# An FFT mixing layer fused with a squared-ReLU feed-forward: FFT units in half-slots of their own, and the read of a z quarter moved ahead of the read of u

## The chip, the cores and the metric

The kernel runs on one core of one Trainium2 chip. The metric is device microseconds of an execution; the time of a version is the median of its runs. A profile records one execution, with the span from its first to its last instruction.

## The reference

The input is `x` of 8 batches, 3008 positions and 256 channels. Per batch the layer computes

```
X = rfft(x, axis=1); y = irfft(X * (filt_r + 1j*filt_i), n=3008, axis=1)
h = relu(y @ w_in)            # 256 -> 2048
out = (h * h) @ w_out         # 2048 -> 256, over all 24064 tokens
```

All inputs and the output are float32; the kernel works in float16 with float32 accumulation.

## The kernel before

The transform of length 3008 is split as 64 x 47. For each batch it has four kinds of unit, each of which fills one PSUM bank on TensorE (PE) and is emptied by another engine:

- `unit_a` (16 per batch, L345): one 512-column matmul of `x` into `psA`, cast to `u` by ScalarE (ACT) or, for odd units of batches 1 and 2, VectorE (DVE). Four units fill a chunk of `u`, which `write_u` sends to DRAM (`dU`).
- `unit_b` (12, L436): two 256-column matmuls of `ut` into `psB`; DVE multiplies by the filter into `prod` (L450), and GpSimd (POOL) issues two DMAs that add one half of `prod` onto the other (L457).
- `unit_p` (12, L480): two 256-column matmuls of `prod` into `psP`, cast to `ze` by ACT (L489). Every third one sends a quarter of `ze` to DRAM (`dZ`, L492).
- `unit_y` (16, L509): four 94-column matmuls of `zt` into `psY`, cast to `yt` by ACT for even units and by DVE for odd ones (L530, L532).

`read_u` (L429) reads the whole of a batch's `dU` back as `ut`, transposed, in a DMA of 512 KB and one of 1024 KB. `read_z` (L501) reads one quarter of a batch's `dZ` in two DMAs of 192 KB, into one of two buffers. The quarters 0 and 1 of `dZ` are written early, so only the second DMA of a read needs the last write of `dZ`. The reads, the writes of `dU` and `dZ` and all stores of the output are issued on one queue, that of SyncE (SP), in program order; an issue that has to wait holds up what is behind it. The loads of `x` (L195) and the additions onto `prod` stand on POOL's queue.

The feed-forward works on groups of 512 tokens, eight slots to a group. In each slot `ffn_g1` makes two of the 16 tiles of `h` (four matmuls of 512 columns into `psH`, L553; ACT applies the ReLU, L557), and DVE squares them two slots' worth at a time (L564, in every odd slot). The second product of the previous group is done in the same slot: for most groups by `products` (L666), a Strassen form of 16 matmuls of 128 columns per slot into `psX` and `psY`, for which DVE makes four sums (L639 to L648, in slots 0, 1, 2 and 4 of a group) and three additions; for the first groups and the last by `ffn_g2` (L573).

The order of all this is written out by hand. The main loop goes over slots and emits, in each: `ffn_g1`, the units of the slot's first half (place 0), `products` or `ffn_g2`, the units of the second half (place 1), then the sums and the square. Which unit stands in which half is decided by `fft_plan(b)`: it gives each unit a position in slots, counted from a first slot of its batch, and rounds it down to a half-slot. Several units may fall into one half-slot. A batch takes 47 to 48 slots, and the batches overlap: while the last units of batch b run, those of b+1 and b+2 have begun.

All four kinds of unit share two PSUM banks, the tag `psF` with two buffers: a unit can start only when the unit two before it has been emptied.

Of the kernel before, what the change touches and what calls it, by code (L numbers as in the profile page):

```python
# [19 lines left out]
TG = 512  # L20
SLOTS = 8
# [89 lines left out]
def kernel(  # L111
# [9 lines left out]
    nc = tc.nc  # L121
    B, S, D = x.shape
# [564 lines left out]
                nc.vector.tensor_add(out=v, in0=o, in1=v)  # L687
                store(g, 0, 2, f["top"])

    def fft_plan(b):  # L690

        plan = {}

        def put(r, f, *a):
            r = int(2 * r)
            plan.setdefault(divmod(r, 2), []).append((f, a))

        d = 0
        if b == 1:
            for n in range(4, 16):  # L700
                put((n if n < 8 else n + 2 if n < 12 else 2 * n - 7) + n % 2 / 2, unit_y, 0, n)
            put(7.5, read_z, 0, 3)
            for k in range(4):
                put((4.5, 5.5, 7.5, 7.5)[k], cast_wout, k, nc.vector)
            for a in range(12, 16):
                put(2 + a / 2, unit_a, b, a)
            put(10.5, read_u, b)
            d = 7
        else:
            for a in range(16):  # L710
                if a % 2 == 0 and b > 2:
                    put((-57 + 2.3 * a) if b == 3 else (-66 + 2.75 * a), load_x, b, a // 2)
                put((-16 + a, -46 + 2.2 * a, -56 + 2.75 * a)[min(b, 4) - 2], unit_a, b, a)
            put(2 if b == 2 else -9, read_u, b)
        for p in range(12):
            r = 14 + 15 * p / 11 if b == 1 else 6 + 28 * p / 11 if b == 2 else -5 + 39 * p / 11
            put(r, unit_b, b, p)
            if b == 1 and 2 <= p < 10:
                put(r, load_x, 2, p - 2)
            put(r + 4.5, unit_p, b, p)  # L720
        for c in range(4):
            put((41, 41.5, 48, 54)[c] - d, read_z, b, c)
        for n in range(16):
            put(YN[n] - d, unit_y, b, n)
        return plan

    YN = (45, 45.5, 46, 46.5, 47.5, 49, 50.5, 52, 54, 56, 58, 60, 63, 66, 69, 72)

    def run(plan, r, place):
        for f, a in plan.get((r, place), ()):  # L730
            f(*a)


# [8 lines left out]
    for k in range(2):  # L742
        c = slice(12 * k, 12 * k + 12)
# [26 lines left out]
    for k in range(6):  # L770
        if k % 3 == 0:
            sSPx.append(p_u.tile([128, 12, 128], F16, tag="u", name=f"sSPx_{k}"))
        c, o = slice(4 * k, 4 * k + 4), slice(4 * k % 12, 4 * k % 12 + 4)
# [27 lines left out]
    read_z(0, 2)  # L801

    SEVEN = range(6, NG - 1)
    work = {}
    for b in range(1, B):
        first = (b * S // TG) * SLOTS - (48 if b > 1 else 40)
        for (r, place), w in fft_plan(b).items():
            work.setdefault((first + r, place), []).extend(w)

    for s in range((NG + 1) * SLOTS):  # L810
        g, k = divmod(s, SLOTS)
        if g < NG:
            ffn_g1(g, k)
        run(work, s, 0)
        if SEVEN[0] * SLOTS <= s < SEVEN[0] * SLOTS + 4:
            make_t(s % SLOTS)
        if (s - 1) // SLOTS - 1 in SEVEN:
            products((s - 1) // SLOTS - 1, (s - 1) % SLOTS)
        if g > 0 and g - 1 not in SEVEN:
            ffn_g2(g - 1, k)  # L820
        run(work, s, 1)
        if g > 0 and g - 1 not in SEVEN:
            ffn_out(g - 1, k)
        if g - 1 in SEVEN:
            sums(g - 1, k)
        if g < NG:
            ffn_sq(g, k)
# [30 lines left out]
```

## Time and profile before

| | |
|---|---|
| median of 6 runs | 786.99 us (785.86 to 788.06) |
| the profiled execution's own time | 787.4 us |
| its span | 785.4 us |
| PE busy | 755.9 us (96%) |
| DVE, ACT, POOL busy | 618.9 (79%), 583.3 (74%), 193.0 us (25%) |
| DMA | 109.21 MB, mean 139 GB/s |
| granted TensorE clock | 1.000 |

In a timeline each line has a start, a duration, the engine, the source line and what is written from what; in brackets stand the idle time before it and what ended that. A table of windows gives the busy time of each engine in each stretch of the span. A wait has the engine and line that waited, what it waited for, and then the total in us, the number of times and the longest. SPq and POOLq are issues of DMAs, not their transfers.

### The profile page before, as it was taken

How to read it: one execution, taken by the hardware profiler on the slowest of the kernel's cores; microseconds unless marked ns; L12 is line 12 of the kernel's file. 1: busy time of each engine (PE TensorE's matmuls, PEld its weight loads, DVE VectorE, ACT ScalarE, POOL GpSimd, SP SyncE). 2: the span in 40 equal slices, each digit the busy share in tenths (PEclk: the TensorE clock that was granted, in tenths of full speed). 3: DMA queues.
4: the chain of work that ended last, by engine and by line, in shares of the span. 5: the costliest groups of instructions: out<-in, count | busy, mean ns of one | idle time of the engine just before them, and what ended most of it. 6: DMA issues, size and time to landing. Idle time of an engine off the chain costs nothing.

```text
span 785.4 us, 19161 instructions
## 1 busy us (share of the span) xinstructions
PE 755.9 (96%) x8022; PEld 553.6 (70%) x8022; DVE 618.9 (79%) x679; ACT 583.3 (74%) x831; POOL 193.0 (25%) x260
## 2 busy tenths in 40 slices
PE   8989999999989999899999999999998999999998
PEld 5846666667767777777768777687776877777776
DVE  5866655579778888888887899779977999878874
ACT  3976767778867887778877887778786777777774
POOL 3801640133213321222221323233311222000000
PEclk9999999999999999999999999999999999999999
DMA  9995896656775547665486554855537533421011
GB/s 364 372 254 161 149 174 182 171 103 117 153 187 128 107 97 185 163 129 100 105 215 133 112 125 98 206 131 115 105 83 189 125 68 77 116 69 55 28 49 61
DMA packets 104942, 109.21 MB, mean 139 GB/s; under 512 B 9640, under 2 KB 93096, under 8 KB 102936
## 3 DMA queue, kind: packets, MB, share of 16 engines
q1 hardware_dynamic: 85704, 87.38, 36.6%
q0 software_dynamic: 19008, 20.43, 19.4%
q8 instruction: 63, 1.03, 0.5%
q10 hardware_dynamic: 144, 0.18, 0.1%
q14 instruction: 23, 0.19, 0.1%
HBM read 58.12 MB, written 48.23 MB: 135 GB/s over the span
## 4 chain that ended last, share of the span: by engine, by line
PE 82%; DMA 6%; DVE 6%; ACT 2%; SPq 2%; issue 1%; ACTq 0%; DVEq 0%
PE psH L553 35%; PE psX L666 16%; PE psY L666 12%; PE psO L573 6%; DMA zt<-dZ 4%; DVE prod L450 3%; PE psA L358 3%; PE psP L487 2%; PE psY L523 2%; PE psB L442 2%; DVE h L564 1%; PE warm L272 1%; ACT h L557 1%; DMA ut<-dU 1%; PE psf L291 1%
## 5 line engine op out<-in xcount | busy, mean ns | idle before, releaser
L557 ACT ACTIVATE h<-psH 128x1024 f16<-128x1024 f32 x376 | 385.0, 1025 | 156.5 <-PE psH L553 152.4
L553 PE MATMUL psH<-yt,sWin 128*128 128x512 f16 (+7 forms) x1728 | 386.7, 351 | 1.5 <-DVE yt L532 0.6
L564 DVE TENSOR_TENSOR h<-h 128x2048 f16<-128x2048 f16 (+1 forms) x192 | 229.7, 1197 | 68.9 <-ACT h L557 68.6
L457 POOL DMA_DIRECT2D prod<-prod x168 | 138.9, 972 | 463.5 <-DVE prod L450 457.5
L553 PEld LDWEIGHTS <-sWin 128*128 128x128 f16 x1728 | 152.8, 98 | 97.0 <-issue 3.8
L666 PEld LDWEIGHTS <-sum 128*128 128x128 f16 x2560 | 158.0, 98 | 25.2 <-issue 1.4
L666 PEld LDWEIGHTS <-h 128*128 128x128 f16 x1920 | 119.1, 98 | 20.5 <-issue 1.4
L450 DVE TENSOR_TENSOR prod<-psB,sF 128x1024 f16<-128x1024 f32 x84 | 102.5, 1220 | 26.6 <-PE psB L442 26.3
L666 PE MATMUL psX<-sT,sum 128*128 128x128 f16 x1280 | 91.0, 219 | 0.0
L666 PE MATMUL psY<-sT,sum 128*128 128x128 f16 x640 | 61.9, 219 | 0.0
L573 PE MATMUL psO<-sWout,h 128*128 128x256 f16 x448 | 56.9, 272 | 0.0
L523 PEld LDWEIGHTS <-zt 112*128 112x128 f16 x512 | 34.1, 98 | 30.0 <-issue 11.0
L532 DVE CAST yt<-psY 128x376 f16<-128x376 f32 x62 | 33.7, 544 | 27.0 <-PE psY L523 26.8
L362 ACT CAST u<-psA 96x512 f16<-96x512 f32 x90 | 52.2, 581 | 2.4 <-PE psA L358 1.9
L573 PEld LDWEIGHTS <-h 128*128 128x128 f16 x448 | 43.2, 98 | 14.8 <-issue 4.5
L489 ACT CAST ze<-psP 128x512 f16<-128x512 f32 x84 | 49.3, 587 | 4.3 <-PE psP L487 4.2
L523 PE MATMUL psY<-sC,zt 112*128 112x94 f16 x512 | 42.4, 205 | 10.3 <-DMA zt<-dZ 10.1
L642 DVE TENSOR_TENSOR sum<-sum,h 128x2048 f16<-128x2048 f16 x40 | 48.9, 1221 | 0.9
L666 PE MATMUL psY<-sWout,h 128*128 128x128 f16 x640 | 48.8, 219 | 0.0
L666 PE MATMUL psX<-sT,h 128*128 128x128 f16 x640 | 48.8, 219 | 0.0
L648 DVE TENSOR_TENSOR sum<-h,sum 128x2048 f16<-128x2048 f16 x40 | 48.6, 1216 | 0.0
L666 PE MATMUL psY<-sWout,sum 128*128 128x128 f16 x640 | 48.6, 219 | 0.0
(86 smaller groups left out, 706.5 us busy)
## 6 DMA issues: line engine op xcount, KB each, us to landing
zt<-dZ SPq DMA_DIRECT2D x64, 192.0 KB
dU<-u SPq DMA_DIRECT2D x28, 384.0 KB
prod<-prod POOLq DMA_DIRECT2D x168, 64.0 KB, 2.8
dZ<-ze SPq DMA_DIRECT2D x28, 384.0 KB
x<-in_x_dram POOLq DMA_DIRECT2D x40, 192.0 KB, 4.7
ut<-dU SPq DMA_DIRECT2D x7, 1024.0 KB
xw<-in_x_dram SPq DMA_DIRECT2D x6, 1024.0 KB
ut<-dU SPq DMA_DIRECT2D x7, 512.0 KB
```

The lines of the kernel that those rows point to most:

```text
L362: nc.scalar.copy(out=o, in_=pv)
L450: nc.vector.tensor_mul(out=prod, in0=ps.rearrange("p (a d) -> p a d", d=D).unsqueeze(1).to_broadcast([128, 2, 2, D]), in1=sF[:, :, 2 * p:2 ...
L457: nc.gpsimd.dma_start(out=prod[64 * i:64 * i + 64, 0], in_=prod[64 - 64 * i:128 - 64 * i, 1], accum_op=mybir.AluOpType.add)
L489: nc.scalar.copy(out=zes[(b, c)][:, 2 * i6:2 * i6 + 2, :], in_=ps.rearrange("p (a d) -> p a d", d=D))
L523: nc.tensor.matmul(ps[:, 94 * jj:94 * jj + 94], zt[:, 4 * (g % 2) + jj, dt * 128:(dt + 1) * 128], sSY, start=True, stop=True)
L553: nc.tensor.matmul(ps[:, i, o:o + n], sWin[:, dt, jt * 128:(jt + 1) * 128], yts[b][:, dt, r:r + n], start=(dt == 0), stop=(dt == 1))
L557: nc.scalar.activation(out=h2[:, 2 * s:2 * s + 2, :], in_=ps, func=AF.Relu)
L564: nc.vector.tensor_mul(out=v, in0=v, in1=v)
L573: nc.tensor.matmul(pso[g][:, t % 2, :], h2s[g][:, jt, t * 128:(t + 1) * 128], sWout[:, jt, :], start=(jt == 0), stop=(jt == NJT - 1))
L642: nc.vector.tensor_sub(out=t, in0=f[5], in1=a11)
L648: nc.vector.tensor_sub(out=t, in0=a12, in1=f[6])
L666: nc.tensor.matmul(o[:, t, :], f[p][:, q, 128 * t:128 * t + 128], sg["w"][p][:, q, :], start=(m == 0 and p in (1, 2)), stop=(q == 7), skip ...
```

## The change

`fft_plan` is called once and makes one list for all batches. For batches 2 to 7:

- Units a, b and p, and units y from the fifth on, get half-slots of their own: they are placed one after the other, kind by kind (b, p, y, a), each in the free half-slot nearest to its wished position, from three half-slots ahead of it on; a half-slot with more than two taken neighbours (of the four nearest) is avoided. The first four y units of every batch, and all but the late y units of batch 1, keep fixed positions.
- The first read of z of a batch goes from position 41 to 40 and the second from 41.5 to 43; the read of the next batch's u goes from -9 to -6.5, which is 39 and 41.5 in the same count. So the order on SP's queue, u, z quarter 0, z quarter 1, becomes z quarter 0, u, z quarter 1. Batch 2's read of u stays at its place, and for batch 1 only the second z read moves, by a slot and a half.
- From batch 3 on the units b and p begin three slots later and end at the same place: 12 products over 36 slots, not 39.
- Small shifts: the a units of batch 3 are spread by 2.1 slots instead of 2.2, and four y positions move by half a slot.

No instruction is added or taken away on the engines; what changes is their order.

```diff
-    def fft_plan(b):
+    YN = (45, 45.5, 46, 46.5, 48, 49.5, 51, 52.5, 54, 56, 58, 60, 63, 66, 69, 72)
+    def fft_plan():
+        fixed, units, moves = [], [], []
+        for b in range(1, B):
+            f = (b * S // TG) * SLOTS - (48 if b > 1 else 40)
...
-                put((-16 + a, -46 + 2.2 * a, -56 + 2.75 * a)[min(b, 4) - 2], unit_a, b, a)
-            put(2 if b == 2 else -9, read_u, b)
+                    units.append((f + (-16 + a, -46 + 2.1 * a, -56 + 2.75 * a)[min(b, 4) - 2],
+                                  unit_a, b, a))
+                moves.append((f + (2 if b == 2 else -6.5), read_u, b))
         for p in range(12):
-            r = 14 + 15 * p / 11 if b == 1 else 6 + 28 * p / 11 if b == 2 else -5 + 39 * p / 11
-            put(r, unit_b, b, p)
...
-            put(r + 4.5, unit_p, b, p)
+                r = 14 + 15 * p / 11 if b == 1 else 6 + 28 * p / 11 if b == 2 else -2 + 36 * p / 11
+                (fixed if b == 1 else units).append((f + r, unit_b, b, p))
...
+                (fixed if b == 1 else units).append((f + r + 4.5, unit_p, b, p))
         for c in range(4):
-            put((41, 41.5, 48, 54)[c] - d, read_z, b, c)
+                moves.append((f + (40 + d / 7, 43, 48, 54)[c] - d, read_z, b, c))
         for n in range(16):
-            put(YN[n] - d, unit_y, b, n)
-        return plan
-    YN = (45, 45.5, 46, 46.5, 47.5, 49, 50.5, 52, 54, 56, 58, 60, 63, 66, 69, 72)
+                (fixed if n < 4 else units).append((f + YN[n] - d, unit_y, b, n))
+        work, used, done = {}, set(), {}
+        for r, *u in fixed:
+            h = int(2 * r)
+            used.add(h)
+            work.setdefault(h, []).append(u)
+        rank = (unit_b, unit_p, unit_y, unit_a)
+        for r, *u in sorted(units, key=lambda u: (rank.index(u[1]), u[0])):
+            after = done.get((u[0], u[1]), -1)
+            h = min((h for h in range(max(int(2 * r) - 3, after + 1), int(2 * r) + 12)
+                     if h not in used),
+                    key=lambda h: (sum(h + i in used for i in (-2, -1, 1, 2)) > 2) * 2
+                    + abs(h - int(2 * r)))
+            used.add(h)
+            done[(u[0], u[1])] = h
+            work.setdefault(h, []).append(u)
+        for r, *u in moves:
+            work.setdefault(int(2 * r), []).append(u)
+        return work
```

More of the change, by code (lines that the diff above doesn't have):

```diff
@@ L688, in products @@
                 store(g, 0, 2, f["top"])
-    def fft_plan(b):
[L692 to L712, printed above, removed]
-                put((-16 + a, -46 + 2.2 * a, -56 + 2.75 * a)[min(b, 4) - 2], unit_a, b, a)
-            put(2 if b == 2 else -9, read_u, b)
-        for p in range(12):
-            r = 14 + 15 * p / 11 if b == 1 else 6 + 28 * p / 11 if b == 2 else -5 + 39 * p / 11
-            put(r, unit_b, b, p)
-            if b == 1 and 2 <= p < 10:
-                put(r, load_x, 2, p - 2)
-            put(r + 4.5, unit_p, b, p)
-        for c in range(4):
-            put((41, 41.5, 48, 54)[c] - d, read_z, b, c)
-        for n in range(16):
-            put(YN[n] - d, unit_y, b, n)
-        return plan
@@ L727 @@
-    YN = (45, 45.5, 46, 46.5, 47.5, 49, 50.5, 52, 54, 56, 58, 60, 63, 66, 69, 72)
-    def run(plan, r, place):
-        for f, a in plan.get((r, place), ()):
+    YN = (45, 45.5, 46, 46.5, 48, 49.5, 51, 52.5, 54, 56, 58, 60, 63, 66, 69, 72)
[3 more added lines that the diff above has]
+            f = (b * S // TG) * SLOTS - (48 if b > 1 else 40)
+            d = 0
+            if b == 1:
+                for n in range(4, 16):
+                    fixed.append(((n if n < 8 else n + 2 if n < 12 else 2 * n - 7) + n % 2 / 2,
+                                  unit_y, 0, n))
+                moves.append((7.5, read_z, 0, 3))
+                for k in range(4):
+                    moves.append(((4.5, 5.5, 7.5, 7.5)[k], cast_wout, k, nc.vector))
+                for a in range(12, 16):
+                    fixed.append((2 + a / 2, unit_a, b, a))
+                moves.append((10.5, read_u, b))
+                d = 7
+            else:
+                for a in range(16):
+                    if a % 2 == 0 and b > 2:
+                        moves.append((f + ((-57 + 2.3 * a) if b == 3 else (-66 + 2.75 * a)),
+                                      load_x, b, a // 2))
+                    units.append((f + (-16 + a, -46 + 2.1 * a, -56 + 2.75 * a)[min(b, 4) - 2],
+                                  unit_a, b, a))
+                moves.append((f + (2 if b == 2 else -6.5), read_u, b))
+            for p in range(12):
+                r = 14 + 15 * p / 11 if b == 1 else 6 + 28 * p / 11 if b == 2 else -2 + 36 * p / 11
+                (fixed if b == 1 else units).append((f + r, unit_b, b, p))
+                if b == 1 and 2 <= p < 10:
+                    moves.append((f + r, load_x, 2, p - 2))
+                (fixed if b == 1 else units).append((f + r + 4.5, unit_p, b, p))
+            for c in range(4):
+                moves.append((f + (40 + d / 7, 43, 48, 54)[c] - d, read_z, b, c))
+            for n in range(16):
+                (fixed if n < 4 else units).append((f + YN[n] - d, unit_y, b, n))
[17 more added lines that the diff above has]
+        return work
@@ L731, in run @@
+    def run(plan, s, place):
+        for f, *a in plan.get(2 * s + place, ()):
             f(*a)
@@ L803 @@
     SEVEN = range(6, NG - 1)
[L804 to L808, printed above, removed]
+    work = fft_plan()
     for s in range((NG + 1) * SLOTS):
```

## The prediction

> **What bounds the kernel now.** I read the page's busy line first, then busy time by stretches of the span.
>
> ```profile
> PE 755.9 (96%) x8022; PEld 553.6 (70%) x8022; DVE 618.9 (79%) x679; ACT 583.3 (74%) x831; POOL 193.0 (25%) x260
> ```
>
> ```profile
> core 0: us, PE busy (x) PEld busy (x) DVE busy (x) ACT busy (x) POOL busy (x), PEclk, DMA share, GB/s
> 0.00:50.00 50.00, 44.04 (x433) 32.68 (x434) 34.39 (x45) 31.49 (x41) 23.77 (x36) 1.00 0.90 334
> 50.00:210.00 160.00, 153.43 (x1277) 104.73 (x1276) 107.11 (x111) 119.35 (x166) 49.88 (x67) 1.00 0.71 158
> 210.00:610.00 400.00, 386.55 (x4347) 288.22 (x4346) 336.06 (x366) 310.24 (x454) 102.87 (x137) 1.00 0.60 137
> 610.00:750.00 140.00, 139.97 (x1628) 103.77 (x1626) 120.34 (x134) 103.06 (x144) 16.44 (x20) 1.00 0.30 75
> 750.00:785.40 35.40, 31.93 (x345) 24.20 (x343) 20.95 (x26) 19.18 (x27) 0.00 (x0) 1.00 0.17 55
> ```
>
> PE is the bound. It idles 6.0 us before 50 us and 3.5 us after 750 us, where the change does nothing. In between it idles 6.57 + 13.45 + 0.03 = 20.05 us: no reordering can win more. The 13.45 us lie in five places. Three more answers, over five stretches of 10 us where two batches meet (from 217, 310, 404, 498 and 592 us), five of 20 us right after them, and four of 60 us for the rest:
>
> ```profile
> sum 50.00, PE 40.98 PEld 29.73 DVE 36.59 ACT 31.58 POOL 11.14; mean PE 8.20 PEld 5.95 DVE 7.32 ACT 6.32 POOL 2.23
> ```
>
> ```profile
> sum 100.00, PE 95.68 PEld 79.61 DVE 86.56 ACT 76.98 POOL 26.43; mean PE 19.14 PEld 15.92 DVE 17.31 ACT 15.40 POOL 5.29
> ```
>
> ```profile
> sum 240.00, PE 239.89 PEld 173.80 DVE 209.66 ACT 193.04 POOL 68.59; mean PE 59.97 PEld 43.45 DVE 52.42 ACT 48.26 POOL 17.15
> ```
>
> So 9.0 us at the seams, 4.3 just after, 0.1 elsewhere. PE's waits say on what:
>
> ```profile
> PE psY L523 <- DMA zt<-dZ: 10.1, 6, 2.6
> PE psP L487 <- DVE prod L450: 3.0, 7, 0.5
> PE psA L358 <- DVE prod L450: 2.8, 11, 0.3
> PE psA L358 <- ACT ze L489: 1.5, 2, 1.2
> PE psA L358 <- ACT yt L530: 1.1, 1, 1.1
> ```
>
> The first line is the seam: the first y unit of a batch waits for its z quarter. The others are not data but banks: a unit waits until the unit two before it has been emptied. The timeline at the third batch's seam, SP and then PE:
>
> ```profile
> 307.12 1.27 SPq L433 DMA_DIRECT2D ut<-dU  x2
> 308.49 1.82 SPq L606 DMA_DIRECT2D out_dram<-bot  x3
> 310.41 0.40 SPq L604 DMA_DIRECT2D out_dram<-top  x1
> 310.86 4.91 SPq L505 DMA_DIRECT2D zt<-dZ  x4
> ```
>
> ```profile
> 318.68 0.33 PE L523 MATMUL psY<-sC,zt 112*128 112x94 f16 x4 [1.44 <-DMA zt<-dZ]
> ```
>
> By size of packet, the 1.5 MB of u move from 309.4 to 314.7 us (5.2 us), and only then, from 315.3, the z reads, whose first 384 KB are over by 317.2. The y unit starts 1.4 us later. Without the wait it would have started at about 317.1 (the gap between PE starts is 1.6 us longer than the matmul before needs).
>
> [...]all of u's packets precede z's. [...]So the second half of the z read, now first, can hold up SP. [...]a bank is emptied no sooner than what stands ahead on its engine; the trace agrees (a square at 329.70 us for 1.22 us, and the product whose psB began at 329.46 starts at 330.83).
>
> **The z read moved ahead.** In the new order on SP's queue stand: last write of dZ, three stores, z quarter 0, one store, u, z quarter 1. The write of dZ is issued at 306.63 us as before; its 512-byte packets are over by 309.4. The z read's second half is released at about 310.3[...] and needs 2 us for 384 KB, as now, plus 1.4 to the y unit: ready at 313.8, wanted at 317.1. So the wait goes, at five seams: **-9.0 us**.
>
> What is late next? The read of u (two issues), one store and z quarter 1 stand behind. u starts at about 312, takes 5.2 and 1.4 us: 318.7. Its first user, unit b 0, has moved from slot 43 to 46 of its batch: after 317.1 come two slots of 0.88 (psH) + 0.89 (products) with four y units of 0.16, and one psH, so 321.3. Cover 2.6 us, and for the first third of u more. z quarter 1 follows u, ready by about 320, wanted at slot 48, some 323. If u were late by x, each seam would lose x; I take 0, ends 0 and 1.5.
>
> **Half-slots of their own.** In the old table 22 units in slots 136 to 183 leave two half-slots or less to the unit that reuses their bank, several one or none; in the new one 18, all exactly two. The waits after the seams come from such pairs: y and p in one half-slot (wait 0.47 us at 324.67), p and a (0.21 at 332.10), y and a (0.27 at 338.50). They go: -4.3 us. New ones: in slot 143 a b unit stands in the second half, in 144 a y unit that DVE casts, and in 145 a p unit that wants the y unit's bank. DVE does the product (1.22), the square (1.22) and the cast (0.55), beginning 0.42 after the b unit: 3.4 us. PE gets from the b unit to the p unit through b 0.21, psH 0.88, y 0.16, products 0.89, a 0.21, psH 0.88: 3.2 us. With a semaphore 0.3 to 0.4 us of wait. DVE is then behind through the sums of slots 0, 1 and 2, and the next b unit (slot 147) is emptied about 0.25 us late. That is 0.65 a batch, five batches: **+3.0 us**, ends 0 and 6. Net of this part **-1.3**.
>
> In 50 to 210 us the idle 6.57 us have much that stays (the start, batch 1's fixed units). PE idles 2.3 us in 92 to 120 and 1.8 in 148 to 165; the larger waits there (1.3 at 109 and 1.2 at 157) are three units in one half-slot, which the list parts. I take **-2.6**, ends -4.5 and 0.
>
> **Products over 36 slots.** DVE's load in a dense stretch is 52.4 of 60 us (87%). The same 12 products in 36/39 of the time add 1 us of 1.22 us products there: 89%. Hidden by DVE's idle; no cost. New is the first p unit, now seven half-slots after its b unit, where all others keep nine: 6.9 us by the old slot starts. From b to the landing: 0.5 + 1.22 (product) + 0.3, 0.56 to the second POOL issue, 2.8 (median) to 4.6 us (at a seam): 5.4 to 7.2. So a wait of 0 to 0.3; by packets the worst old case is 8.3, behind the u read. I take 0, ends 0 and 1.4 a batch. SP, POOL and the loads of x keep their counts; x is loaded 15 half-slots or more before its use.
>
> **Sum.** -9.0 - 1.3 - 2.6 = -12.9: the profiled span 785.4 becomes 772.5, its own time 787.4 becomes 774.5. The median stands 0.4 below that execution: 774.0 us.
>
> **Rivals.** (1) The seam wait only changes hands: u late for b 0, the first p unit on its landing, or a worse queue on DVE. For: SP is now held by the write of dZ, with u behind; against: 2.6 us of cover. At 1.5 us a seam that gives back 7 us: 781. (2) The moved z read doesn't help, since the write of dZ is the late one. It would take a landing 3.3 us later than reckoned, near 313; its packets are gone by 309.4. Then only the half-slots work: about 783. (3) Slower: the first p unit of batches 3 to 7 waits for the addition onto prod. Place: PE at slot 50 of a batch, with ffn_g1 and all else queued behind. Its price is five times what the landing exceeds 6.9 us; it eats the gain of 13 us from 2.6 us on, a landing 9.5 us after the b unit. The longest now is 8.3. At 4 us a batch: 794.
>
> **From these to numbers.** Forecast 0.65 (its own range 768 to 778); rival 1 0.20, rival 2 0.05, both faster unless they combine; 0.02 for no change; rival 3 and its like 0.08. A measurement of this kernel tells 0.2% (1.6 us) from nothing. Faster 0.89, same 0.02, slower 0.09. Low end: with no new bank waits and all early waits gone, -9.0 - 4.3 - 4.5 = -17.8, 769; taken as 768. High end 781, by rival 1.
>
> **What would show it.** Right: no wait of psY on zt at the seams; PE's idle in the middle from 20 to about 7 us; u's packets after the first z read's; psH starts at a seam about 2 us apart throughout. Wrong: psB waiting for ut, psP waiting for prod by DMA, or psP and psY waiting for DVE's yt and prod casts in slots 143 to 148 of each period by more than 1 us. If DVE or ACT proves to be the pace once PE no longer stalls, the dense stretches will show PE below 60 of 60 us, and the prediction fails there.

## The result

| | before | after |
|---|---|---|
| median | 787.65 us (69 runs) | 784.36 us (32 runs) |
| lowest and highest | 784.46 to 792.19 us | 780.41 to 790.37 us |
| profiled execution, its span | 787.4, 785.4 us | 780.41, 778.6 us |
| mean granted clock, median of the runs that list it | 0.998 (54 runs) | 0.993 |

The ratio is 0.9956, with a 95% interval of 0.9945 to 0.9967: the change makes the kernel 0.44% faster, 3.3 us. Forecast were 13 us and a range up to 781; the direction was right, the size was not. The table holds two clues. The span of the profiled execution fell by 6.8 us, twice what the median gained. And this execution has a clock of 0.998, while the median run of the changed kernel has 0.993. At one clock, 0.998, the mean span falls from 785.8 us (17 runs) to 778.8 (2 runs); at 0.993 the changed kernel's is 782.9 (13 runs). So the order is worth about 7 us, and the lower clock takes some 4 of them back.

The profile after: the page's busy line, then busy time by stretches of the span.

```profile
PE 754.0 (97%) x8022; PEld 553.5 (71%) x8022; DVE 620.8 (80%) x679; ACT 578.8 (74%) x831; POOL 192.7 (25%) x260
```

```profile
50.00:210.00 160.00, 156.53 (x1325) 107.67 (x1324) 109.29 (x115) 122.78 (x172) 50.37 (x68) 1.00 0.74 164
210.00:610.00 400.00, 388.82 (x4400) 291.66 (x4398) 342.26 (x369) 307.76 (x457) 102.33 (x137) 1.00 0.59 136
```

In 50 to 210 us PE idles 3.5 us instead of 6.6, but in 210 to 610 still 11.2 (13.45 before). The same three sets of stretches as before, moved to where the seams now lie (from 212, 304, 398, 491 and 584 us; the 20 us after each; the four of 60 us):

```profile
sum 50.00, PE 50.00 PEld 36.38 DVE 40.80 ACT 39.27 POOL 0.00; mean PE 10.00 PEld 7.28 DVE 8.16 ACT 7.85 POOL 0.00
```

```profile
sum 100.00, PE 89.60 PEld 76.04 DVE 82.87 ACT 69.18 POOL 27.63; mean PE 17.92 PEld 15.21 DVE 16.57 ACT 13.84 POOL 5.53
```

```profile
sum 240.00, PE 239.22 PEld 172.83 DVE 212.53 ACT 191.27 POOL 76.09; mean PE 59.80 PEld 43.21 DVE 53.13 ACT 47.82 POOL 19.02
```

The seams themselves are now without a gap: 50.00 of 50 us, where PE was busy for 40.98. The loss has moved into the 20 us behind them: 10.4 us, where it was 4.3. PE's waits name it:

```profile
PE psP L487 <- DMA prod<-prod: 10.4, 5, 2.7
PE psP L487 <- DVE prod L450: 2.0, 7, 0.6
PE psY L523 <- DMA zt<-dZ: 1.9, 2, 1.0
PE psA L358 <- ACT yt L530: 0.3, 1, 0.3
```

psY's 10.1 us on zt have become 1.9, and psA's 5.4 us on banks 0.3. In their place stands a wait that the kernel before didn't have: five p units, one a batch, wait for the additions onto `prod`. The timeline at the seam that the prediction looked at shows one of them, first SP's issues and then the first b unit of the new batch and what bears on its p unit:

```profile
301.97 1.45 SPq L606 DMA_DIRECT2D out_dram<-bot  x3
303.52 0.85 SPq L505 DMA_DIRECT2D zt<-dZ  x2
304.46 0.40 SPq L604 DMA_DIRECT2D out_dram<-top  x1
304.95 0.95 SPq L433 DMA_DIRECT2D ut<-dU  x2
```

```profile
314.97 0.38 PE L442 MATMUL psB<-ut,sSB 128*128 128x256 f16 x2
315.39 1.22 DVE L450 TENSOR_TENSOR prod<-psB,sF 128x1024 f16<-128x1024 f32 x1 [0.16 <-PE psB L442]
316.48 0.40 SPq L604 DMA_DIRECT2D out_dram<-bot  x1
316.91 1.69 POOL L457 DMA_DIRECT2D prod<-prod  x2 [19.48 <-DVE prod L450]
316.98 0.41 SPq L341 DMA_DIRECT2D dU<-u  x1
317.48 2.19 SPq L505 DMA_DIRECT2D zt<-dZ  x2
324.49 0.38 PE L487 MATMUL psP<-prod,sSP 128*128 128x256 f16 x2 [2.72 <-DMA prod<-prod]
```

The z read is issued first and u behind it, as intended. The p unit starts 9.5 us after its b unit; without the wait it would have started 6.6 us after. Between the two lie a store of 256 KB, the write of 384 KB of the next u in 512-byte packets and a read of 384 KB of z, all issued within a microsecond of the additions. The additions' last packet is over at 322.9, 1.6 us before the p unit starts.

The other clue was the clock. The stretch of 3.4 us behind this wait, against the next:

```profile
325.50:328.90 3.40, 3.40 (x27) 2.85 (x26) 1.23 (x1) 1.97 (x3) 0.00 (x0) 0.50 0.11 20
329.00:332.40 3.40, 3.40 (x49) 3.07 (x48) 2.32 (x3) 2.19 (x3) 0.26 (x1) 1.00 0.39 116
```

The last but two column is the granted clock. In the first line it is 0.50, and PE gets through 27 matmuls instead of 49, though it is "busy" throughout. The clock records of this profile have one such slow stretch before PE's last matmul: it begins at 325.50 us, 1.0 after the start of the p unit, and is 3.41 us long; at half rate it costs 1.7 us. By this length a whole stretch lowers the mean clock of 780 us by 0.0022, so the median run with 0.993 has about three of them, by estimate.

### The profile page after: what moved, and what is told of

It reads as the page before. It is cut to its first block, busy times and chain, and to the rows that moved or that the text cites. A ratio compares the mean times of both kernels' runs of the same rounds, so it can differ in the third digit from the quotient of the medians.

```text
span 778.6 us, 19169 instructions
## 1 busy us (share of the span) xinstructions
PE 754.0 (97%) x8022; PEld 553.5 (71%) x8022; DVE 620.8 (80%) x679; ACT 578.8 (74%) x831; POOL 192.7 (25%) x260
## 4 chain that ended last, share of the span: by engine, by line
PE 82%; DVE 7%; DMA 6%; ACT 2%; issue 1%; POOL 0%; ACTq 0%; SPq 0%; DVEq 0%
PE psH L553 36%; PE psX L666 17%; PE psY L666 12%; PE psO L573 6%; DMA prod<-prod 4%; DVE prod L450 3%; PE psP L487 2%; PE psB L442 2%; PE psA L358 2%; PE psY L523 2%; DVE h L564 2%; PE warm L272 1%; DMA zt<-dZ 1%; ACT h L557 1%; PE psf L291 1%
## 5 line engine op out<-in xcount | busy, mean ns | idle before, releaser
L645 DVE TENSOR_TENSOR sum<-h 128x2048 f16<-128x2048 f16 x40 | 48.6, 1216 | 0.0
L639 DVE TENSOR_TENSOR sum<-h 128x2048 f16<-128x2048 f16 x40 | 48.6, 1214 | 0.0
```

The source lines that it names most:

```text
L639: nc.vector.tensor_add(out=t, in0=a21, in1=a22)
L645: nc.vector.tensor_sub(out=t, in0=a11, in1=a21)
```

## The experiments

Theory A: the gain was lost to the first p unit of each batch from 3 to 7, which the list placed seven half-slots behind its b unit, where all others of these batches have nine; the rest of the change works. (The first b unit is wished in slot 46, but the fixed y units hold the half-slots there, so the list puts it in 47, four slots later than before and not three. The first p unit finds its wished half-slot free, and so comes two closer.) Rival B: the order works, but a PE that idles less is granted less clock. Rival C: the additions are late by themselves, wherever the unit stands.

**Every p unit nine half-slots behind its b unit.**

```diff
+            if u[0] is unit_p:
+                after = max(after, done[(unit_b, u[1], u[2])] + 8)
             h = min((h for h in range(max(int(2 * r) - 3, after + 1), int(2 * r) + 12)
...
-            done[(u[0], u[1])] = h
+            done[(u[0], u[1])] = done[tuple(u)] = h
```

> The changed kernel with one rule more: no p unit stands closer than nine half-slots behind its own b unit, so the first p unit of batches 3 to 7 moves from seven to nine half-slots; all DMAs keep their places. Theory A (the changed kernel lost its gain to this p unit, which waits 10.4 us in five batches for the additions onto prod): two half-slots are about 1.9 us, so of the waits of 2.3, 2.9, 2.5, 2.1 and 1.4 us some 2 us in all are left; the span falls by 8 to 9 us against the changed kernel's 778.6 at the same clock, to about 770, and the median stands about 1.1% under the changed kernel's. Rival B (with PE busier the granted clock falls, and takes back what the order wins): the waits go as under A, but the mean granted clock falls below the changed kernel's 0.988 to 0.998 and the time stays within 0.3% of it. Rival C (the landing follows the p unit, since the traffic moves with it): the wait on prod stays near 10 us.

770.83 us median, 0.9787 of the kernel before (0.9766 to 0.9807), span 769.1; the clock of its runs is 0.998 to 1.000. PE's waits:

```profile
PE psY L523 <- DMA zt<-dZ: 2.7, 2, 1.6
PE psP L487 <- DVE prod L450: 2.1, 7, 0.6
PE psP L487 <- DMA prod<-prod: 1.9, 2, 1.0
```

Theory A holds: the waits left and the span came out as expected. The median fell by more than the 1.1% expected, 1.8% against the changed kernel's runs on the same chip. Two half-slots for five units are worth 14 us of the median: 8.4 us of waits, and the slow stretches, which go with them. The list then also moves a y unit and two a units of most batches by a slot or so, but the waits of all other units stay as they were (5.0 and 5.2 us, in the ledger below). Rival B falls: this kernel keeps PE busier than the two before it and has the higher clock. Rival C falls too: in this profile the additions are as late as in the changed kernel (last packet up to 7.9 us after the b unit), but only 1.9 us of waiting for them are left.

**The reads and the 36 slots without the list.** The kernel before, with only these three lines.

```diff
-            put(2 if b == 2 else -9, read_u, b)
+            put(2 if b == 2 else -6.5, read_u, b)
...
-            r = 14 + 15 * p / 11 if b == 1 else 6 + 28 * p / 11 if b == 2 else -5 + 39 * p / 11
+            r = 14 + 15 * p / 11 if b == 1 else 6 + 28 * p / 11 if b == 2 else -2 + 36 * p / 11
...
-            put((41, 41.5, 48, 54)[c] - d, read_z, b, c)
+            put((40 + d / 7, 43, 48, 54)[c] - d, read_z, b, c)
```

> The old table, in which units may share a half-slot, with the read of z quarter 0 ahead of the read of u and with products over 36 slots; p units all nine half-slots behind their b units. This is the change without the list. Theory A: the seam's waits of PE on zt (10.1 us before, of which about 9 at the five seams) go, the bank waits after the seams (4.3 us) stay, and no p unit waits long for prod: PE idle in the middle falls from 20 to about 11 us, and the time by 9 us, 1.1%, against the kernel before at the same clock. Rival B (clock): the span of the profile falls, but the mean clock of the timed runs is below that of the runs of the kernel before by what the waits win, and the median moves by less than 0.5%.

778.89 us, 0.9889 (0.9868 to 0.991), clock 1.0: 8.8 us, as expected. Among PE's longer waits there is none of psP for `prod` by DMA. The first b unit stands one slot earlier, before the store and the write of u are issued, and the last packet of the additions comes 4.8 to 5.1 us after it, not 6.8 to 8.0.

**The list alone.** The first experiment with the reads at their old places and 39 slots.

```diff
-                moves.append((f + (2 if b == 2 else -6.5), read_u, b))
+                moves.append((f + (2 if b == 2 else -9), read_u, b))
...
-else -2 + 36 * p / 11
+else -5 + 39 * p / 11
...
-(40 + d / 7, 43, 48, 54)[c]
+(41, 41.5, 48, 54)[c]
```

> The list with the nine half-slot rule of the first experiment, but the reads at their old places (u ahead of z) and products over 39 slots. This is the list alone. Theory A: the seam waits on zt stay (9 to 10 us), the bank waits after the seams and those in 92 to 165 us go: 4.3 less about 2 new ones and about 3 of the early ones, 4 to 6 us, 0.5 to 0.8% under the kernel before at the same clock. Rival B (clock): the mean clock of the timed runs falls with it, and the median moves by less than 0.3%.

775.55 us, 0.9844 (0.9823 to 0.9865): 12.1 us, twice to three times the 4 to 6 expected. The seam wait is still there, as it should be, and nearly all the bank waits are gone:

```profile
PE psY L523 <- DMA zt<-dZ: 8.3, 7, 1.7
PE psP L487 <- DVE prod L450: 1.0, 3, 0.4
```

So the list, with nine half-slots for p, is worth more than the reads. The two don't add up to the first experiment (8.8 + 12.1 against 16.8 us). The list alone already shortens the seam waits, from 9.8 to 6.8 us at the five seams; and each of the three gains contains the slow stretch that the median run of the kernel before has (below), 1.7 us by estimate.

**The changed kernel again,** on the chip of the three above.

> The changed kernel itself, on the same chip as the three others, for its clock and its waits. Under theory A its profile shows about 10 us of psP waiting for prod by DMA again, and its median stands 0.4% under the kernel before and about 1% above the first experiment. Under rival B its mean clock lies below that of the kernel before by 0.3% or more, and the spans of its runs follow the clock: about 779 us at 0.998 and 785 at 0.991.

785.13 us, 0.9959 (0.9939 to 0.998). The p waits are the same, 10.3 us in 5; the clock of its runs is 0.991 to 0.996. Its clock records have four slow stretches, one at 50 us and three behind p waits, and its span is 783.7 us. Here a stretch and the one behind it, with the matmuls of one line alone:

```profile
326.20:329.60 3.40, 1.91 (x8) 1.22 (x8) 0.50 0.42 74
329.60:333.00 3.40, 1.93 (x16) 1.50 (x16) 1.00 0.20 47
```

Eight of psH's matmuls in the first, sixteen in the second.

**The write of u moved away from the additions.** The first p unit stays at seven half-slots. The fourth a unit, which sends the chunk of u, goes from slot 47.5 of the batch in front to 53: eleven half-slots, not the five of the expectation.

```diff
+                    late = 3.5 if b > 3 and a == 3 else 0
-                    units.append((f + (-16 + a, -46 + 2.1 * a, -56 + 2.75 * a)[min(b, 4) - 2],
-                                  unit_a, b, a))
+                    units.append((f + (-16 + a, -46 + 2.1 * a, -56 + 2.75 * a)[min(b, 4) - 2]
+                                  + late, unit_a, b, a))
```

> The changed kernel, with the first p unit still seven half-slots behind its b unit, but the fourth a unit of batches 4 to 7 some five half-slots later, so that the write of its chunk of u (384 KB in 512-byte packets, issued in the changed kernel at the moment when the two additions onto prod are issued) goes out after that p unit. Theory A1 (the write of u lengthens the additions): the last packet of the first b unit's additions comes some 6 us after its matmul instead of 7.7 to 8.0, the wait of psP on prod falls from 10.3 us to 2 to 4, and the median falls by 7 us or more. Theory A2 (the stores and the z read do it, or the additions are just slow there): the packets stay at 7.5 or more, the wait at 8 us or more, the median within 2 us of the changed kernel's 785.

775.86 us, 0.9852 (0.9827 to 0.9877), 9.3 us under the changed kernel's 785.13.

```profile
PE psP L487 <- DMA prod<-prod: 6.5, 6, 1.7
```

The additions come earlier, but by less than expected: last packet 7.3, 7.2, 6.9 and 6.4 us after the b unit of batches 3 to 6, against 8.0, 8.0, 7.7 and 7.7; the wait is 6.5 us in 6, not 2 to 4. So the write of u is one cause of the late landing. Batch 7 says the same without an edit: no batch comes after it, so no u is written at its seam, and in the changed kernel its last packet comes after 6.8 us. The rest, against the 4.8 us of the second experiment, lies with what else is issued then, the stores and the z read, or with something that was not separated. The median falls by more than the wait, since no slow stretch is left in the profile (clock 0.997 to 1.000).

**The first p unit at five half-slots.**

```diff
-            h = min((h for h in range(max(int(2 * r) - 3, after + 1), int(2 * r) + 12)
+            r -= (u[0] is unit_p and u[1] > 2 and u[2] == 0)
+            h = min((h for h in range(max(int(2 * r) - (0 if u[0] is unit_p else 3), after + 1),
+                                      int(2 * r) + 12)
```

> The changed kernel with the first p unit of batches 3 to 7 at five half-slots behind its b unit instead of seven, all else as near as the list allows. The unit then wants prod some 1.9 us earlier, so each of the five waits grows from about 2.1 to about 4 us: 9 us more. Theory A with the clock (a wait of PE of two or three microseconds can be followed by a stretch of 3.4 us at half clock, which costs 1.7 us more; the two profiles of the changed kernel show one and three such stretches after five waits): after waits of 4 us nearly every one is followed by one, so 2 to 4 more stretches than in the changed kernel, 3 to 7 us on top; the mean clock of the timed runs falls from 0.991 to 0.988 or less and the median stands 11 to 16 us above the changed kernel's 785, near 798. Rival (the slow stretches have nothing to do with the waits): the clock stays at 0.991 to 0.998 and the median is 9 us above.

797.17 us, 1.0121 (1.01 to 1.0143), clock 0.985 to 0.987.

```profile
PE psP L487 <- DMA prod<-prod: 19.8, 5, 4.6
```

The waits grew by 9.5 us, and the time by 12; the ledger below has 3.9 us more of slow stretches than in the changed kernel's second profile. Each of the five waits (3.2 to 4.8 us from matmul to matmul) is followed by one. The profile's mean clock is 0.987, lower by what six lengths of 3.41 us take, so one of the five lasted two lengths, by estimate.

**Nine half-slots, and the write of u late.** Both edits together.

> The first experiment (nine half-slots for every p unit) with the fourth a unit later as well: a candidate for the best version. Theory A: the 1.9 us that psP still waits for prod in the first experiment go, no other wait grows by more than 0.5 us; the span is 767 to 768.5 and the median 769 to 770, 0.1 to 0.3% under the first experiment's 770.8. Rival: a later a unit pushes others onto banks that are not free yet, and the time is the same or a little longer.

769.02 us, 0.9768 (0.9746 to 0.9791), span 767.2: the lowest median of the study, 2.3% under the kernel before. One p wait of 1.0 us for the additions is left.

**The kernel before again.**

> The kernel before, for the clock of its runs. If waits of two microseconds and more bring slow stretches, its runs show them too (its longest waits on zt are 2.6 and 2.3 us): mean clocks between 0.993 and 1.000, with the time following, about 785.5 at 1.000 (787.4 with what lies around the span) and 1.7 us more for each stretch. If the slow stretches belong to the changed kernel alone, all clocks are 0.999 or more.

788.43 us, 1.0002 (0.9985 to 1.0019). Its clocks are 0.995 to 1.000, so by 0.0022 a stretch it has slow stretches too, about one in the median run and none to two in the others (its two profiles happen to have none). They don't belong to the changed kernel alone.

**The reads swapped, but 39 slots.** The first experiment with `-5 + 39 * p / 11`.

> The first experiment (list, nine half-slots for p, z quarter 0 read ahead of u), but with products over 39 slots as before, so that the first b unit of batches 3 to 7 stands four slots earlier, in slot 43 of the batch in front. It asks whether the three slots' later start belongs to the swap of the reads. Theory A (it does): in the changed kernel's profile the packets of u's first third are over at about 309 us and the b unit would start at 307.4 in that slot, so with a microsecond and a half of completion each of the five b units waits for ut for about 3 us, 15 us in all, and such waits bring a stretch at half clock in most seams (1.7 us each, mean clock 0.988 to 0.993): the median is 788 to 796 instead of 770.8. Rival (u is in time at slot 43 too, and the later start was not needed): no wait of psB on ut above 0.5 us, and the median is 769 to 773.

790.02 us, 1.0029 (1.0012 to 1.0045), clock 0.987 to 0.993: 0.3% slower than the kernel before.

```profile
PE psB L442 <- DMA ut<-dU: 14.5, 5, 3.3
```

The first b unit waits for u, and each of its five waits is followed by a slow stretch (the profile's mean clock is 0.989, five times 0.0022 below 1). The microsecond and a half that the expectation puts between a last packet and the start that it releases is what two profiles show: 1.6 us at the changed kernel's seam above (322.9 and 324.49 us), 1.4 in the kernel before (317.2 and 318.68). So the later start of the b units is not a matter of taste: it belongs to the swap of the reads.

## Why the prediction was wrong

The first p unit's wait, which the prediction put at nothing, measured 11.2 us. To see it beside the other terms, take the time between the starts of two matmuls, less what a matmul of the first one's size takes where nothing is waited for (512 columns: 0.216 us from start to start, the median in the profile before). This excess, counted from 60 us on where it is over 30 ns, gives one ledger for all profiles. "Slow" is what the matmuls of slow stretches take longer.

| us | z at the seams | first p of a batch | u | other waits | slow |
|---|---|---|---|---|---|
| before | 9.8 | 0 | 0 | 15.8 | 0 |
| after | 0 (1.1 in batch 1) | 11.2 | 0 | 5.0 | 1.6 |
| after again | 0 (0.9 in batch 1) | 11.1 | 0 | 6.1 | 5.0 |
| nine half-slots | 0 (1.2 in batch 1) | 2.3 | 0 | 5.2 | 0 |
| reads, 36 slots | 0 | 0 | 0 | 17.6 | 0 |
| list alone | 6.8 (1.4 in batch 1) | 0 | 0 | 4.5 | 0 |
| write of u late | 0 (0.9 in batch 1) | 6.9 | 0 | 5.3 | 0 |
| first p unit at five | 0 (0.9 in batch 1) | 20.6 | 0 | 5.0 | 8.9 |
| nine, and write of u late | 0 (1.2 in batch 1) | 1.2 | 0 | 5.0 | 0 |
| reads, 39 slots | 0 (0.8 in batch 1) | 0 | 15.3 | 4.8 | 8.1 |

**The z read moved ahead, -9.0 us:** right. 9.8 us went, also in the experiment without the list (8.8 us of median). The z read's second half, which could have held up SP, did not: its two issues took 0.85 us, and the second began at 303.99 us, 0.6 after the last packet of the write of dZ (303.40), where 0.9 was reckoned. What was reckoned late next, u, was in time: no psB waited. Its cover was larger than the 2.6 us reckoned for the whole of u: the last experiment takes four slots away, 7.6 us at this seam, and gets five waits of 2.9 us in the mean, so the cover was between 4 and 5 us, by estimate.

**Half-slots of their own, -1.3 and -2.6 us:** right in kind, too small by a factor of near three. Other waits fell by 10.8 us, not 3.9. Two terms were mis-sized. The waits were read off PE's busy time, where a matmul's modelled end (0.38 us for a unit's last) reaches over the start of what could follow 0.22 us later (in the profile after, the psA of 315.86 us is given 0.38, and psH starts at 316.08), so that each short wait shows 0.16 us too little: 20.05 us of idle in the middle were really 25.6. And the new DVE waits in slots 143 to 148 were put at 0.65 us a batch, which for five batches makes 3.25 us, not the 3.0 of the sum. Of the two waits named, only the second is there, a p unit in slot 148 of each period that wants the bank of the b unit in 147: 0.36 us in batches 3 to 6 and 0.8 in the last. The p unit in slot 145 doesn't wait. And a semaphore was to turn the 0.2 us between 3.4 and 3.2 into 0.3 to 0.4; in the profile before, PE started 0.053 to 0.058 us after the end of the DVE instruction that released it, in 24 waits.

**Products over 36 slots, no cost for DVE:** right; it is busy for 53.1 of 60 us in the dense stretches, where 89% was said.

**The first p unit at seven half-slots, 0 to 0.3 us a batch, taken as 0:** this step failed. It cost 1.4 to 2.9 us a batch, 11.2 in all. It was named and priced, and given to the third rival at 0.08, but its terms were taken from the wrong traffic. The distance, 6.9 us, came out as 6.6. The landing was put at 5.4 to 7.2 us after the b unit, from issues of the kernel before; the p unit could start only after 7.9 to 9.5. Two things were missed. The worst row of the kernel before, 8.3 us, was for the last packet, and in the changed kernel the p unit starts 0.9 to 1.6 us after it. And the change moves units, and with them the DMAs that units issue: the fourth a unit, which sends a chunk of u, came to stand in the half-slot right behind the first b unit. The prediction counted the moved reads, but not the moved write; to send it later is worth 9.3 us of the median, slow stretches included.

**The clock** was in no step. The new waits are 1.4 to 2.9 us long, and behind some of them PE runs at half rate: one slow stretch in the first profile, three behind p waits in the second. By the mean clock of 0.993 the median run has about three, at 1.7 us each, where the median run before has one. That is why the median gained only half of what the order is worth. What sets the clock was not shown; the last section has what came behind waits of which length.

Without this one defect the changed kernel takes 770.8 us, less than the 774 that were forecast: the gain of the parts that worked was set too low, and what ate it was set at nothing. That the direction came out right is in part luck. The half-slots gave 6.9 us more than reckoned; with the reckoned 3.9 us the changed kernel would have stood near 791, by estimate, above the kernel before.

## What to carry to other kernels

Where a transfer's issue hangs on a unit of work, moving the unit moves the transfer: list the DMAs of every moved unit, the writes too, next to the waits with the least cover. A minimum distance between a producer and the consumer of its transfer belongs into the placement as a constraint, not as a wish that a nearest-free search may cut short. And one wait of two to three microseconds on PE can cost more than four of half a microsecond, since here it was at times followed by 3.4 us at half clock: read the clock of the timed runs beside their times.

## What had not been expected

The slow stretches after short waits. The longest waits of PE in each profile, from matmul to matmul and from 60 us on, and how many of them were followed by one:

| profile | waits, us | followed by a slow stretch |
|---|---|---|
| before | 2.76, 2.33 | none |
| before again | 2.53 | none |
| after | 2.05, 2.31, 2.54, 2.89 | one, the last |
| after again | four, 2.09 to 2.87 | three |
| first p unit at five | five, 3.2 to 4.8 | all |
| reads, 39 slots | five, from 2.7 up | all |
| the other five | none of 2 us or more | none |

No wait under 2 us was followed by one, and of those from 2.05 to 2.9 us in the kernel before and the changed one some were and some were not. The length alone does not settle which: 2.76 us in the kernel before was not followed by half clock, while the shortest of the last experiment, 2.7 us, was. What settles it was not shown.

The runs differ in the same way. The mean clocks of the last experiment's 20 runs are 0.987 to 0.993, most of them 0.989 or 0.991, and those of the changed kernel's second set 0.991, 0.993 and 0.996: steps of about 0.0022, which is one slow stretch. So executions of one kernel seem to differ by whole stretches, by estimate from the length of the one at 325.50 us; the timed runs have no trace to show it.
